# Closing a kernel's context behind its first three loads, and clearing its semaphores during the last store

## The chip, the cores and the metric

The kernel runs on one core of a Trainium2 chip. The metric is the device time of one execution, in microseconds. The core has five engines with a queue of instructions each: TensorE (PE in the profile; its weight loads are PEld), VectorE (DVE), ScalarE (ACT), GpSimd (POOL) and SyncE (SP). They run independently and wait for each other by semaphores, which are counters that one instruction raises and another waits for. SP and ACT issue transfers between the chip's memory and the on-chip buffers; 16 DMA engines carry them out, and each finished transfer raises a semaphore by 16.

## The reference: one decoding step of gated attention beside a gated feed-forward layer

One token with 512 features goes through an attention block that reads a cache of 32768 positions, and through a feed-forward block; a scalar gate mixes the two. All numbers are float32.

```
g   = sigmoid(sum(x * gate_w))                        # x: 1 x 1 x 512
q   = (x @ wq) as 32 heads of 128                     # wq: 512 x 4096
a   = softmax(q . k_cache * 128**-0.5) . v_cache      # 8 cached heads x 32768 x 128, four query heads share one
a   = a as 1 x 4096 @ wo                              # wo: 4096 x 512
b   = (silu(x @ w1) * (x @ w3)) @ w2                  # w1, w3: 512 x 1792, w2: 1792 x 512
out = g * a + (1 - g) * b                             # 1 x 1 x 512
```

The two caches are 134 MB each, the five weight matrices together 28 MB. Each is read once.

## The kernel before, in words

**Buffers.** Three large on-chip buffers, `ra`, `rb` and `rc`, hold 128 x 16384 numbers each (8.39 MB). They are reused in turn: first `rc` takes `wq`, `rb` takes `w1` and `w3`, and `ra` takes the first half of the first head's keys. Then `ra` and `rb` take the key halves of the eight heads and `rc` the value halves. At the end `ra` and `rb` take the last head's values, `rc` takes `wo`, and `ra` takes `w2` in four pieces.

**Loads.** All large loads are issued by SP, in the order in which they stand (lines 118 to 152). The first five (118 to 122) wait for nothing; line 124 waits until the feed-forward rows have read `rb` (the counter `c_e`), line 128 until the scores of the first key half are done (`c_k`), and so on. ACT issues the two small loads of `x` and `gate_w` (155, 156), a store of zeros to the output (162), and at the very end the store of the result (460). Both stores raise `l_out`.

**Work.** PE turns `x` into columns (187), computes the gate's sum (196), the queries (202) and the rows of the feed-forward layer (229). A loop over eight heads follows on PE and on DVE: DVE transposes keys (342), PE multiplies them with the queries (271), ACT takes the exponentials (386), PE multiplies with the values (285). The helper `take` (112) waits for a semaphore and lowers it again. Behind the loop come the products with `wo` (421) and `w2` (428, 438), the copies of the result (456), and the store.

**The frame.** The launch (lines 468 to 489) opens a context (485) and calls the kernel inside it. The kernel puts the whole program into one critical section of that context (line 27), inside which it sets all semaphores itself. The context and the section put instructions of their own around the program. In the profile they carry the line numbers 476 (the start of the program: every engine reports and is let go by POOL), 27 (the entry and the exit of the section) and 485 (a branch at the entry, and the end of the context: drains, semaphore instructions by which all engines report and are let go, and one instruction that clears a range of semaphores). A drain waits until an engine's earlier instructions are through. The last instruction of the program itself is line 461: POOL waits until both stores have landed.

Of the kernel before, what the change touches and what calls it, by code (L numbers as in the profile page):

```python
# [3 lines left out]
F32 = mybir.dt.float32  # L4
# [5 lines left out]
P = 128  # L10
# [13 lines left out]

@with_exitstack
def kernel(ctx, tc, x, k_cache, v_cache, wq, wo, w1, w3, w2, gate_w, out):
    with tc.tile_critical(sync_engine=mybir.EngineType.Activation, no_gpsimd_drain=True):
        _program(tc.nc, x, k_cache, v_cache, wq, wo, w1, w3, w2, gate_w, out)


def _program(nc, x, k_cache, v_cache, wq, wo, w1, w3, w2, gate_w, out):
    pe, dve, act, pool, sp = nc.tensor, nc.vector, nc.scalar, nc.gpsimd, nc.sync
    _, HKV, S, DH = k_cache.shape
    D = x.shape[-1]
    F = w1.shape[1]
    HQ = wq.shape[1] // DH
    REP = HQ // HKV
    NC = D // P
# [4 lines left out]
    W = NK * DH  # L43
    assert DH == P and D == 4 * P and REP == 4 and HKV == 8 and NK == 128 and F == FR * P

    def sb(name, *shape):
        return nc.alloc_sbuf_tensor(name, [P, *shape], F32).ap()

    def token(name):
        return nc.alloc_semaphore(name)  # L50

    def count(name):
        return Count(nc, name)


    ra, rb, rc = sb("ra", W), sb("rb", W), sb("rc", W)

    ident, ones, fold, dmask = sb("ident", P), sb("ones", P), sb("fold", 32), sb("dmask", 4)
    xp = sb("xp", NC, 32)
# [25 lines left out]
    def bank(n, w=1):  # L85
# [4 lines left out]
    pq = [bank(3), bank(4)]  # L90


    l_x, l_q = token("l_x"), token("l_q")
    l_a, l_a2, l_b, l_c = token("l_a"), token("l_a2"), token("l_b"), token("l_c")
    l_w1, l_w3 = token("l_w1"), token("l_w3")
    l_v = [token(f"l_v{i}") for i in range(2)]
    l_wo = [token(f"l_wo{i}") for i in range(2)]
    l_w2 = [token(f"l_w2{i}") for i in range(4)]
    l_out = token("l_out")

    c_q, c_k, c_v, c_e = (count(n) for n in ("c_q", "c_k", "c_v", "c_e"))
    c_nm, c_act, c_pool, done = token("c_nm"), count("c_act"), count("c_pool"), count("done")

    t_f, t_m, t_n, t_h, t_r, t_l = (token(n) for n in ("t_f", "t_m", "t_n", "t_h", "t_r", "t_l"))
    d_s = token("d_s")

    t_x, t_tr, t_win, t_ev, t_ob, t_mx, t_md, t_p, t_e = (
        token(n) for n in ("t_x", "t_tr", "t_win", "t_ev", "t_ob", "t_mx", "t_md", "t_p", "t_e")
    )

    def take(sem, n=1, engine=pe):
        engine.wait_ge(sem, n).then_inc(sem, -n)  # L112
# [2 lines left out]
    kd = k_cache.rearrange("a h (p m n) d -> (a h) m p (n d)", p=P, m=2, n=NK)  # L115
    vd = v_cache.rearrange("a h (r p n) d -> (a h) r p (n d)", r=2, p=P, n=NK)
    half = W // 2
    sp.dma_start(rc, wq.rearrange("(p c) n -> p (c n)", c=NC)).then_inc(l_q, 16)
    sp.dma_start(rb[:, 0:NC * F], w1.rearrange("(p c) f -> p (c f)", c=NC)).then_inc(l_w1, 16)
    sp.dma_start(rb[:, NC * F:2 * NC * F], w3.rearrange("(p c) f -> p (c f)", c=NC)).then_inc(l_w3, 16)  # L120
    sp.dma_start(ra[:, 0:half], kd[0, 0][:, 0:half]).then_inc(l_a, 16)
    sp.dma_start(ra[:, half:W], kd[0, 0][:, half:W]).then_inc(l_a2, 16)
    sp.wait_ge(c_e.sem, 2)
# [27 lines left out]
    for i in range(4):  # L151
# [17 lines left out]
        out=ident, in_=ident, compare_op=ALU.not_equal, fill=1.0, base=0, pattern=[[-1, P]], channel_multiplier=1,  # L169
# [256 lines left out]
    for k in range(W2[1]):  # L426
        t = k % 4
        i = pe.matmul(  # L428
            acc[32 * t:32 * t + 32, :], htp[:, k, :], w2t[:, k, :], start=False, stop=(k >= W2[1] - 4),
            skip_group_check=True,  # L430
        )
# [22 lines left out]
    for j in range(4):  # L454
        copy = act.copy if j % 2 else dve.tensor_copy
        i = copy(row[:, j * P:(j + 1) * P], pb[32 * j:32 * j + 1, 0:P])  # L456
# [1 line left out]
            done.by(i)  # L458
    act.wait_ge(done.sem, done.n)
    act.dma_start(od, row).then_inc(l_out, 16)  # L460
    c_pool.by(pool.wait_ge(l_out, 32))


# [26 lines left out]
```

## Time and profile before

| What | Value |
|---|---|
| median of 3 runs | 694.0 us (693.97 to 694.11) |
| the profiled execution | 694.02 us |
| its span, from the first to the last instruction of the program | 691.9 us |
| DMA queue of SP (q1) | 296.23 MB, 99.2% of 16 engines' span |
| mean rate over the span | 428 GB/s |
| busy: PE, DVE, ACT, POOL | 53%, 44%, 6%, 1% of the span |
| granted TensorE clock, mean | 0.785 |

In the rows shown below, times are microseconds from the span's start unless marked ns. A row of the timeline has the start, the duration, the engine, the line, the operation, what is written from what, the count, and in brackets the idle time before it with what ended it. A row of a line has the engine, the operation and the count, then the shortest, middle and longest duration in ns, and the starts of the first and the last. A small q behind an engine's name means its queue: drains, branches, semaphore instructions and the issue of a transfer, none of which counts as busy time. A row of stretches has start and end, the length, the busy time of each engine with its number of instructions, the granted TensorE clock, the mean busy share of the DMA engines and the rate.

### The profile page before, as it was taken

The numbers are of one execution on the slowest core, as the hardware profiler recorded it, in microseconds if no ns is written. First come the engines' busy times: TensorE is split into PE (matmuls) and PEld (weight loads), VectorE is DVE, ScalarE is ACT, GpSimd is POOL, SyncE is SP. The second block draws the span as 40 slices with busy tenths as digits, with TensorE's granted clock in tenths as the row PEclk, the third lists the DMA queues.
The fourth block names the chain that finished last, engine by engine and source line by source line (L and its number), as shares of the span: only waits on it lengthen the run. The fifth ranks groups of instructions, "written<-read, shape, count | busy, mean of one in ns | idle before, by whom it ended". The sixth has DMA issues, their size and how long they took to land. (4 is left out here: it accounts for less than half of the span.)

```text
span 691.9 us, 6738 instructions
## 1 busy us (share of the span) xinstructions
PE 368.2 (53%) x2952; PEld 107.5 (16%) x2952; DVE 307.0 (44%) x194; ACT 41.6 (6%) x111; POOL 7.0 (1%) x41
## 2 busy tenths in 40 slices
PE   1636255467463734466573735466463734466567
PEld 1100011103010121103010211103010211103122
DVE  1019378291725447091825446191816356181000
ACT  0020011002000010002000010001000010001000
POOL 0000000000000000000000000000000000000000
PEclk9975598868686977779577967888786966798678
DMA  9999999999999999999999999999999999999996
GB/s 383 421 439 454 424 429 425 447 447 424 425 432 432 436 447 436 424 424 432 432 440 451 428 424 428 436 428 443 447 424 424 432 432 436 447 436 424 424 423 291
DMA packets 6078, 296.35 MB, mean 428 GB/s; under 512 B 691, under 2 KB 691, under 8 KB 950
## 3 DMA queue, kind: packets, MB, share of 16 engines
q1 hardware_dynamic: 6048, 296.23, 99.2%
q8 instruction: 6, 0.10, 0.1%
q14 instruction: 2, 0.02, 0.0%
q10 hardware_dynamic: 22, 0.01, 0.0%
HBM read 296.23 MB, written 0.00 MB: 428 GB/s over the span
## 5 line engine op out<-in xcount | busy, mean ns | idle before, releaser
L342 DVE STREAM_TRANSPOSE rb<-rb 128x2048 f32<-128x2048 f32 x64 | 141.8, 2275 | 150.3 <-DVEq L112 150.3
L342 DVE STREAM_TRANSPOSE ra<-ra 128x2048 f32<-128x2048 f32 x64 | 141.4, 2275 | 43.6 <-DVEq L112 43.6
L271 PE MATMUL psum<-rb,winbuf 128*32 128x512 f32 x512 | 88.2, 766 | 130.2 <-PEq L112 130.2
L285 PE MATMUL psum<-rc,prob 128*32 128x512 f32 x896 | 111.2, 653 | 42.5 <-PEq L112 42.5
L271 PE MATMUL psum<-ra,winbuf 128*32 128x512 f32 x512 | 85.2, 764 | 86.7 <-PEq L112 86.7
L285 PEld LDWEIGHTS psum<-rc,prob 128*32 128x32 f32 x896 | 33.5, 120 | 115.5 <-issue 115.3
L366 DVE TENSOR_REDUCE mx<-psum 128x4 f32<-128x1024 f32 x8 | 9.8, 1224 | 81.6 <-DVEq L112 81.6
L271 PEld LDWEIGHTS psum<-rb,winbuf 128*32 128x32 f32 x512 | 13.1, 120 | 203.7 <-issue 203.7
L380 ACT COPY sbuf<-psum 128x512 f32<-128x512 f32 x16 | 9.8, 616 | 477.0 <-PE psum L271 477.0
L271 PEld LDWEIGHTS psum<-ra,winbuf 128*32 128x32 f32 x512 | 14.7, 121 | 150.1 <-issue 150.1
L386 ACT ACTIVATE prob<-psum,nm 128x256 f32<-128x256 f32 x32 | 18.8, 694 | 39.6 <-DVE nm L374 39.6
L295 PE MATMUL psum<-ident,sbuf 128*64 128x64 f32 x512 | 16.7, 223 | 0.8 <-PEq L112 0.8
L295 PEld LDWEIGHTS psum<-ident,sbuf 128*64 128x64 f32 x512 | 15.6, 138 | 7.6 <-issue 7.6
L347 DVE SCALAR_TENSOR_TENSOR otall<-psum,gate,recip 128x4 f32 (+1 forms) x8 | 1.7, 213 | 33.1 <-DVEq L112 33.1
L202 PE MATMUL psum<-rc,xp 128*32 128x512 f32 x64 | 9.8, 783 | 9.2 <-DMA rc<-in_A_wq_dram 9.2
L285 PE MATMUL psum<-rb,prob 128*32 128x512 f32 x64 | 8.4, 684 | 9.8 <-DMA rb<-in_A_v_cache_dram 9.8
L421 PE MATMUL psum<-rc,oq 128*32 128x512 f32 x64 | 10.7, 829 | 2.5 <-DMA rc<-in_A_wo_dram 2.1
L258 POOL COPY winbuf<-winraw 32x16 f32<-32x16 f32 x32 | 6.1, 189 | 537.2 <-PE psum L271 499.6
L285 PE MATMUL psum<-ra,prob 128*32 128x512 f32 x64 | 9.5, 761 | 3.7 <-DMA ra<-in_A_v_cache_dram 3.7
L229 PE MATMUL psum<-rb,xp 128*32 128x448 f32 x64 | 8.4, 683 | 5.6 <-DMA rb<-in_B_w_dram 5.6
L214 DVE STREAM_TRANSPOSE rc<-psum 128x512 f32<-128x512 f32 x2 | 1.3, 696 | 18.7 <-PE psum L202 18.7
L305 PE MATMUL psum<-fold,ob 128*128 128x4 f32 x64 | 8.4, 255 | 0.8 <-PEq L112 0.8
(62 smaller groups left out, 80.6 us busy)
## 6 DMA issues: line engine op xcount, KB each, us to landing
ra<-in_A_k_cache_dram SPq DMA_DIRECT2D x2, 4096.0 KB, 53.3
rc<-in_A_wo_dram SPq DMA_DIRECT2D x2, 4096.0 KB, 45.9
rb<-in_B_w_dram SPq DMA_DIRECT2D x2, 3584.0 KB, 34.7
ra<-in_B_w_dram SPq DMA_DIRECT2D x1, 1536.0 KB, 32.8
ra<-in_B_w_dram SPq DMA_DIRECT2D x1, 1024.0 KB, 35.0
ra<-in_B_w_dram SPq DMA_DIRECT2D x1, 768.0 KB, 36.3
ra<-in_B_w_dram SPq DMA_DIRECT2D x1, 256.0 KB, 36.5
rc<-in_A_v_cache_dram SPq DMA_DIRECT2D x14, 30.6
```

The lines of the kernel that those rows point to most:

```text
L202: m = pe.matmul(pq[b][32 * j:32 * j + 32, :], xp[:, c, :], rc[:, o:o + REP * DH], start=(c == 0), stop=(c == NC - 1),)
L229: i = pe.matmul(ps[32 * j:32 * j + 32, 0:FJ], xp[:, c, :], rb[:, o:o + FJ], start=(c == 0), stop=(c == NC - 1))
L258: pool.tensor_copy(winbuf[32 * r:32 * r + 32, 16:144].rearrange("p (c k) -> p c k", k=32)[:, :, 4 * r:4 * r + REP], winraw[32 * r:32 * r + ...
L271: i = pe.matmul(s_ps[m][32 * g:32 * g + 32, :], winbuf[:, w:w + 32], region.rearrange("p (n c i) -> p c n i", c=4, i=32)[:, c, n:n + 16], ...
L285: i = pe.matmul(o_ps[32 * t:32 * t + 32, :], prob[:, w:w + 32], region[:, n * DH:(n + 4) * DH], start=(r == 0 and g == 0 and f == 0), stop ...
L295: i = pe.matmul(pf[64 * s:64 * s + 64, 64 * a:64 * a + 64], sbuf[:, a].rearrange("p i m -> p (i m)"), ident.rearrange("p (gf r s q) -> p s ...
L305: i = pe.matmul(mb[:, 0:REP], ob[:, b * P:(b + 1) * P], fold[:, 4 * b:4 * b + 4], start=(b == 0), stop=(b == 3))
L342: dve.transpose(part[:, c], part[:, c]).then_inc(t_tr, 1)
L366: dve.tensor_reduce(mx, pf.rearrange("p (a q) -> p q a", q=REP), axis=AX.X, op=ALU.max).then_inc(t_mx, 1)
L380: act.copy(sbuf[:, :, :, m], s_ps[m].rearrange("p (n i) -> p n i", i=32)).then_inc(t_ev, 1)
L386: act.activation(prob[:, 0:1024].rearrange("p (a n q) -> p n a q", a=16, q=REP)[:, :, :, q], pf.rearrange("p (n a q) -> p n a q", n=16, q= ...
L421: pe.matmul(acc[32 * t:32 * t + 32, :], oq[:, k:k + 32], rc[:, k * D:(k + 1) * D], start=(k < 4), stop=False, skip_group_check=True,)
```

## The change

The context no longer encloses the program. The kernel allocates `rb` and `rc` and three semaphores, issues the loads of `wq`, `w1` and `w3` on SP, and closes and compiles the context at that point; these loads are marked as carrying no semaphore of the context itself. The program follows outside the context, with no critical section. It begins with the load of the first keys. At the end ACT signals `t_end` once it has issued the store; POOL waits for that, clears and frees all semaphores but `l_out`, and then waits for `l_out` and lowers it by 32.

```diff
 @with_exitstack
 def tile_gated_mix_decode_kernel(ctx, tc, x, k_cache, v_cache, wq, wo, w1, w3, w2, gate_w, out):
-    with tc.tile_critical(sync_engine=mybir.EngineType.Activation, no_gpsimd_drain=True):
-        _program(tc.nc, x, k_cache, v_cache, wq, wo, w1, w3, w2, gate_w, out)
-
-
-def _program(nc, x, k_cache, v_cache, wq, wo, w1, w3, w2, gate_w, out):
+    nc = tc.nc
+    rb, rc = (nc.alloc_sbuf_tensor(n, [P, 16384], F32).ap() for n in ("rb", "rc"))
+    l_q, l_w1, l_w3 = (nc.alloc_semaphore(n) for n in ("l_q", "l_w1", "l_w3"))
+    loads = [(rc, wq, l_q)]
+    n = w1.shape[0] * w1.shape[1] // P
+    loads += [(rb[:, i * n:(i + 1) * n], w, sem) for i, (w, sem) in enumerate(((w1, l_w1), (w3, l_w3)))]
+    for to, w, sem in loads:
+        i = nc.sync.dma_start(to, w.rearrange("(p c) n -> p (c n)", p=P)).then_inc(sem, 16)
+
+        tc.no_tile_sem_insts.add(i.ins.name)
+    tc.close()
+    tc.compile()
+    _program(nc, rb, rc, l_q, l_w1, l_w3, x, k_cache, v_cache, wq, wo, w1, w3, w2, gate_w, out)
+
+
+def _program(nc, rb, rc, l_q, l_w1, l_w3, x, k_cache, v_cache, wq, wo, w1, w3, w2, gate_w, out):
...
+    before = nc.snapshot_sems()
+
+
+    ra = sb("ra", W)
...
-    l_x, l_q = token("l_x"), token("l_q")
+    l_x = token("l_x")
     l_a, l_a2, l_b, l_c = token("l_a"), token("l_a2"), token("l_b"), token("l_c")
-    l_w1, l_w3 = token("l_w1"), token("l_w3")
...
-    l_out = token("l_out")
...
-    d_s = token("d_s")
+    d_s, t_end = token("d_s"), token("t_end")
...
+    owned = nc.allocated_since(before)
+    l_out = token("l_out")
...
-    sp.dma_start(rc, wq.rearrange("(p c) n -> p (c n)", c=NC)).then_inc(l_q, 16)
-    sp.dma_start(rb[:, 0:NC * F], w1.rearrange("(p c) f -> p (c f)", c=NC)).then_inc(l_w1, 16)
-    sp.dma_start(rb[:, NC * F:2 * NC * F], w3.rearrange("(p c) f -> p (c f)", c=NC)).then_inc(l_w3, 16)
     sp.dma_start(ra[:, 0:half], kd[0, 0][:, 0:half]).then_inc(l_a, 16)
...
     act.wait_ge(done.sem, done.n)
     act.dma_start(od, row).then_inc(l_out, 16)
-    c_pool.by(pool.wait_ge(l_out, 32))
+
+
+    act.wait_ge(done.sem, done.n).then_inc(t_end, 1)
+    pool.wait_ge(t_end, 1)
+    nc.clear_and_free_semaphores([l_q, l_w1, l_w3, *owned])
+    take(l_out, 32, pool)
```

More of the change, by code (lines that the diff above doesn't have):

```diff
@@ L53, in count @@
         return Count(nc, name)
-    ra, rb, rc = sb("ra", W), sb("rb", W), sb("rc", W)
+    before = nc.snapshot_sems()
+    ra = sb("ra", W)
     ident, ones, fold, dmask = sb("ident", P), sb("ones", P), sb("fold", 32), sb("dmask", 4)
```

## The prediction

> **What bounds the kernel now.** I read the page first: span, busy shares, the slices, the queues.
>
> ```profile
> span 691.9 us, 6738 instructions
> PE 368.2 (53%) x2952; PEld 107.5 (16%) x2952; DVE 307.0 (44%) x194; ACT 41.6 (6%) x111; POOL 7.0 (1%) x41
> DMA  9999999999999999999999999999999999999996
> q1 hardware_dynamic: 6048, 296.23, 99.2%
> q8 instruction: 6, 0.10, 0.1%
> ```
>
> No engine is busy for much over half of the span, while SP's queue (q1) fills 99.2% of the time of all 16 DMA engines: 296.23 MB of weights and cache are read once. So the kernel is a stream. Its time is the time before the first packet, then the stream, then what follows the last packet. The second view, busy time by stage, says where the stream is whole:
>
> ```profile
> core 0: us, PE busy (x) PEld busy (x) DVE busy (x) ACT busy (x) POOL busy (x), PEclk, DMA share, GB/s
> 0.00:4.00 4.00, 0.00 (x0) 0.00 (x0) 1.14 (x5) 1.23 (x1) 0.99 (x9) 1.00 0.81 263
> 4.00:42.00 38.00, 16.12 (x110) 5.94 (x114) 3.61 (x7) 4.64 (x19) 0.76 (x4) 0.96 0.99 427
> 42.00:62.00 20.00, 11.14 (x64) 1.98 (x56) 11.69 (x7) 0.00 (x0) 0.00 (x0) 0.66 1.03 444
> 62.00:120.00 58.00, 28.75 (x209) 6.38 (x213) 40.24 (x22) 4.88 (x11) 0.76 (x4) 0.74 1.00 431
> 120.00:660.00 540.00, 287.94 (x2355) 84.53 (x2347) 249.03 (x150) 29.21 (x77) 4.55 (x24) 0.78 1.00 433
> 660.00:689.20 29.20, 24.24 (x222) 8.71 (x222) 0.70 (x3) 1.17 (x2) 0.00 (x0) 0.83 0.91 386
> 689.20:691.90 2.70, 0.00 (x0) 0.00 (x0) 0.56 (x2) 0.52 (x2) 0.00 (x0) 1.00 0.00 1
> ```
>
> The DMA share is 0.99 to 1.03 from 4 us to 660 us: there is no hole that the change could fill, so what happens between the first loads and the last ones is worth nothing unless it opens a hole. The first 4 us and the last 2.7 us are what the change can touch; in the last 2.7 us the DMA engines do nothing (share 0.00) and the other engines work for half a microsecond. I read the end from the chain of waits, the timeline, the lines of the closing instructions, and the waits of the queue engines, one view after the other:
>
> ```profile
> 687.09 2.12 PE psum L438 x68
> ```
> ```profile
> 689.85 0.21 ACTq L460 DMA_DIRECT2D out_dram<-prob  x1
> ```
> ```profile
> L461 POOLq EVENT_SEMAPHORE  x1: 17/17/17, 691.0 to 691.0; - x1
> ```
> ```profile
> L27 ACTq EVENT_SEMAPHORE  x3: 17/38/38, 690.1 to 690.5; - x3
> L27 ACTq DRAIN  x1: 158/158/158, 690.2 to 690.2; - x1
> ```
> ```profile
> L485 SPq EVENT_SEMAPHORE  x4: 17/22/73, 690.2 to 691.8; - x4
> L485 POOLq EVENT_SEMAPHORE  x4: 17/17/17, 691.2 to 691.7; - x4
> L485 POOLq DRAIN  x3: 34/41/64, 691.1 to 691.6; - x3
> L485 PEldq EVENT_SEMAPHORE  x2: 51/51/51, 691.4 to 691.8; - x2
> L485 POOLq EVENT_SEMAPHORE_RANGE_CLEAR  x1: 71/71/71, 691.5 to 691.5; - x1
> ```
> ```profile
> SPq L485 <- POOLq L27: 0.7, 1, 0.7
> ```
>
> The last matrix products end at 689.2, the store is issued at 689.85, and POOL sees it landed at 691.0 (L461): the store covers about 1.1 us. Only then comes what line 485, the end of the context, has: three drains on POOL, two rounds in which every engine reports and is let go, and between them one clear of the semaphores (71 ns). SP stands 0.7 us for POOL in the meantime. From 691.0 to the span's end at 691.9 nothing of the program's work is done.
>
> **The change part by part.** The sum is made against the profiled execution, 694.02 us, of which 691.9 is span and 2.1 lies outside; the median of the three runs is 694.0, so nothing need be converted.
>
> *The end.* The closing goes from behind the store. What follows the store's landing is one POOL instruction, the wait that also takes the 32 back (17 ns, as L461 has it now, in the same place). Saved: 691.9 - 691.0 = 0.9 us. The rows round to a tenth, so 0.8 to 1.0.
>
> *The clear under the store.* ACT signals t_end behind the issue of the store, in the place where it has a semaphore instruction at 690.1 now; nothing is queued behind that wait on ACT. POOL waits for it, and behind POOL's wait stand the clear and the last wait. By the rows above a drain on each side of the clear costs at most 64 ns and the clear 71: about 0.2 us, twice that if the numbers fall into two ranges. POOL is through by 690.3 to 690.6, and the store lands at 691.0. I cost it at nothing; the cover is the store, and without it the price is 0.2 to 0.4 us.
>
> *The start of the stream.* The lines of the first microsecond, and behind them the timeline:
>
> ```profile
> L476 SPq EVENT_SEMAPHORE  x1: 17/17/17, 0.7 to 0.7; - x1
> ```
> ```profile
> L27 ACTq NOP  x1: 18/18/18, 0.7 to 0.7; - x1
> ```
> ```profile
> L485 SPq COMPARE_BRANCH  x1: 33/33/33, 0.8 to 0.8; - x1
> ```
> ```profile
> 0.92 0.37 SPq L118 DMA_DIRECT2D rc<-in_A_wq_dram  x1
> 0.97 0.53 ACTq L155 DMA_DIRECT2D ob<-in_A_x_dram  x1
> 1.54 0.73 ACTq L156 DMA_DIRECT2D prob<-in_gate_w_dram  x1
> 1.82 0.42 SPq L120 DMA_DIRECT2D rb<-in_B_w_dram  x1
> 2.29 0.53 SPq L121 DMA_DIRECT2D ra<-in_A_k_cache_dram  x1
> 10.74 2.02 PE L187 MATMUL psum<-ones,ob 1*128 1x1 f32 x8 [10.74 <-DMA prob<-in_gate_w_dram]
> 13.11 0.55 PE L196 MATMUL psum<-gsm,ones 1*128 1x1 f32 x2 [0.35 <-PEq L112]
> 22.82 7.69 PE L202 MATMUL psum<-rc,xp 128*32 128x512 f32 x44 [9.15 <-DMA rc<-in_A_wq_dram]
> 41.30 5.27 PE L229 MATMUL psum<-rb,xp 128*32 128x448 f32 x32 [5.64 <-DMA rb<-in_B_w_dram]
> ```
>
> SP is let go by the launch's own barrier at 0.7 (L476), takes a branch at 0.8 that ACT's NOP of line 27, the entry of the section, releases, and issues the first load at 0.92. Outside the section that release is gone; the branch may stay. The load can come between 0.72, right behind the barrier, and 0.92 as now: a gain of 0 to 0.2, and a loss of 0.1 if the context's own entry puts one more branch there. I take 0.1, the middle of the gain, since either end needs one of the two instructions wholly gone or wholly kept. As the stream has no hole up to 660, an earlier first packet is an earlier last one.
>
> *The closing at the front.* It is now paid behind the third load. SP ends that issue at 1.82 + 0.42 = 2.24, less 0.1; the two rounds with the clear cost 0.9 as at the end; so every engine starts on the rest at about 3.0. SP's fourth load goes from 2.29 to about 3.1. Cover: the three loads hold 8.39 + 3.67 + 3.67 = 15.7 MB, 37 us at 427 GB/s; 0.8 us costs nothing. The drains do not wait for the loads: at the end ACT's drain took 158 ns at 690.2 with its store in flight until 691.0. ACT's two small loads go from 0.97 and 1.54 to about 3.0 and 3.6, DVE's and POOL's constants with them. PE then has x at 12.8 instead of 10.74 and is done with the gate at 15.7 instead of 13.66, against the landing of wq at 22.82: of 9.15 us of idle time 2.1 go. Should the small loads take twice their 9.2 us (1.54 to 10.74) because the stream is now ahead of them, PE starts on wq about 2 us late. What is late next is SP's queue:
>
> ```profile
> 46.64 0.33 SPq L124 DMA_DIRECT2D rb<-in_A_k_cache_dram  x1
> 71.06 0.33 SPq L128 DMA_DIRECT2D ra<-in_A_k_cache_dram  x1
> ```
>
> The first five loads are 24.1 MB, 56.5 us, so they last until about 58, and L124 is issued at 46.64, 12 us ahead; its 8.39 MB last until about 78, and L128 is issued at 71.06, 7 us ahead. Two microseconds fit into both. Price: nothing; ends 0 and 2.
>
> *The rest.* Fewer entries of the section, other semaphore numbers, rb and rc allocated ahead of ra: no row shows a price of an address or a number, and I take none.
>
> Sum: 694.02 - 0.9 - 0.1 = 693.0 us, 0.14% less.
>
> **The rivals.**
>
> *The time outside the span shrinks too.* All five engines now leave together at 691.8, the last semaphore rows of line 485. After the change PE is done at 689.2, ACT and POOL at 690.9 at the latest. 2.1 us lie outside the span; if part of it is work that each engine does by itself after its last instruction, and the slow one is PE (51 ns for a semaphore instruction against 17 on POOL), the end moves by more than POOL's: by up to the 1.6 us that PE is now ahead of POOL, half of the 2.1 at most if half lies behind the span. I price it at 0.4 to 1.1: 691.9 to 692.6, middle 692.3. For it speaks that nothing holds the four engines any longer; against it, that no row shows what the 2.1 us are. The Trainium skill, "Runtime: NRT & Kernel Launch", section "The ~15µs preamble/postamble breakdown", has a barrier behind the kernel in which all engines are waited for, about 1.5 us, ahead of the reset of the semaphores: by that rule the early engines would wait for POOL, nothing more is gained, and the time stays 693.0. The profile shows no instruction of it.
>
> *The closing waits for the loads.* This is the way to a slower kernel. If the context's end holds the engines until the three loads have landed, the barrier opens at 42 us: the second half of L229, the third load's reader, starts at 41.30, and the closing takes 0.9. SP issues its fourth load then, 2 us behind the end of the three (about 2 + 37), and refilling the queue takes about 1 (the first load is issued at 0.92, and by the share of 0.81 0.8 of the first 4 us is empty): 3 us lost. x is asked for at 42, and from x to the issue of L124 lie 36 us now (10.74 to 46.64), of which the waits for the first and the third load (9.15 and 5.64) would be gone: about 21. So L124 would come at 42 + 21 and 2 to 9 for x, 65 to 72, where the fourth and fifth load are through at 43 + 20 = 63: another 3 to 10. Together 6 to 13 lost, 1 gained: 699 to 706, middle 702. It decides from the point where the barrier opens more than about 9 us late, past PE's idle time before wq, and more than 7 past that. For it speaks that a context's end is a place of waits; against it, that the loads are marked as carrying none of the context's own semaphores, and the ACT drain above.
>
> *A code fetch falls on the last load.* Six packets of q8 bring instructions: 0.1% of 16 x 691.9 us is 11 us, 1.8 each (0.9 to 2.8 with the rounding), on one DMA engine that then delivers its share of the stream late. The closing's instructions now stand ahead of PE's work, so each fetch comes a few instructions earlier. If one moves onto the engine that brings the last part of w2, the end is 1.8 later: 694.8. The Trainium skill's "Runtime: NRT & Kernel Launch", section "Instruction fetch mechanics", gives blocks of 16 KiB, 256 instructions; q8's six packets with 0.10 MB agree, and a shift of a few in 256 then leaves nearly every fetch at the same work.
>
> *It doesn't do what it says*: leaving the launch's block still runs a closing. Then the end stays and 694.0 remains.
>
> **How the numbers follow.** About 0.2% (1.4 us) is what a measurement of this kernel can tell from no change. Forecast as summed: 46%, at 693.0, own range 692.7 to 693.4, which is within 0.2%. More gained outside the span: 33%, 691.9 to 692.6, faster by over 0.2%. Closing waits for the loads: 10%, slower. Code fetch: 7%, of which 5 within 0.2% and 2 slower. Nothing done: 4%, within. So faster 0.33, within 0.55, slower 0.12. The range from 691.9 to 694.1 holds the forecast, the first rival and the last, 83%.
>
> **What would show it.** Right: the span ends with POOL's wait at about 690.9, no row of line 485 or of the clear behind the store's landing, span 690.9; the first load at 0.8; the barrier rows at 2.2 to 3.0; PE at x near 13 and still idle before wq; the DMA share 0.99 or more from 4 to 660. The first rival: the run's time minus its span clearly under 2.1. The second: barrier rows at 40, a hole in the DMA shares there. The third: the stage behind 660 longer with L438 later against the stream. What would make me wrong most likely is the time outside the span, of which the trace of before shows nothing.

## The result, and the profile after

The changed kernel takes 692.67 us (median of 18 runs, 692.47 to 692.90) against 694.01 for the kernel before, a ratio of 0.9981 with a 95% interval of 0.9974 to 0.9987: 1.34 us less. The forecast was 693.0. The profiled execution took 692.64 us.

The page, and the stages where the stream must show a hole if there is one (columns as in the prediction):

```profile
span 690.7 us, 6722 instructions
q1 hardware_dynamic: 6048, 296.23, 99.3%
q8 instruction: 6, 0.10, 0.1%
```
```profile
4.00:42.00 38.00, 16.00 (x114) 6.07 (x118) 3.85 (x9) 5.87 (x19) 0.76 (x4) 0.94 0.99 427
42.00:62.00 20.00, 11.46 (x60) 1.75 (x52) 12.14 (x7) 0.00 (x0) 0.00 (x0) 0.69 1.03 444
62.00:120.00 58.00, 29.13 (x217) 6.60 (x221) 40.39 (x23) 4.89 (x11) 0.76 (x4) 0.76 1.00 431
120.00:660.00 540.00, 294.60 (x2350) 84.70 (x2339) 248.42 (x149) 29.27 (x77) 4.55 (x24) 0.76 1.00 433
```

The DMA shares and rates are those of before to the last digit: nothing changed in the middle. The start, first the lines of the closing (line 38 now), then the timeline:

```profile
L38 POOLq EVENT_SEMAPHORE  x4: 17/17/17, 2.3 to 2.7; - x4
L38 SPq DRAIN  x3: 7/7/122, 2.1 to 2.5; - x3
```
```profile
0.73 0.37 SPq L34 DMA_DIRECT2D rc<-in_A_wq_dram  x1
1.16 0.90 SPq L34 DMA_DIRECT2D rb<-in_B_w_dram  x2
2.84 0.33 SPq L131 DMA_DIRECT2D ra<-in_A_k_cache_dram  x1
2.86 0.52 ACTq L165 DMA_DIRECT2D ob<-in_A_x_dram  x1
3.42 0.73 ACTq L166 DMA_DIRECT2D prob<-in_gate_w_dram  x1
```
```profile
15.33 2.02 PE L197 MATMUL psum<-ones,ob 1*128 1x1 f32 x8 [15.33 <-DMA prob<-in_gate_w_dram]
17.71 0.55 PE L206 MATMUL psum<-gsm,ones 1*128 1x1 f32 x2 [0.35 <-PEq L125]
22.81 9.26 PE L212 MATMUL psum<-rc,xp 128*32 128x512 f32 x64 [4.55 <-DMA rc<-in_A_wq_dram]
```

The first load is issued at 0.73 instead of 0.92. Behind the third load come the two rounds of the closing, done at 2.8, with no clear between them; then everything else starts. x is there at 15.33 instead of 10.74, and PE still stands 4.55 us for wq and begins on it at 22.81, as before. The end, from the timeline and the lines:

```profile
689.51 0.21 ACTq L470 DMA_DIRECT2D out_dram<-prob  x1
```
```profile
L475 POOLq DRAIN  x1: 110/110/110, 689.8 to 689.8; - x1
L475 POOLq EVENT_SEMAPHORE_RANGE_CLEAR  x1: 265/265/265, 690.0 to 690.0; - x1
```
```profile
L125 POOLq EVENT_SEMAPHORE  x1: 17/17/17, 690.6 to 690.6; - x1
```

The store is issued at 689.51, POOL drains and clears at 689.8 to 690.3, and the wait for the store passes at 690.6, 1.1 us behind its issue as before. It is the last instruction: the closing that filled 691.0 to 691.9 is gone. In these two executions the store is issued 0.34 us earlier (689.51 against 689.85), more than the first load's 0.19; the rest is the size of what single executions differ by, whose spans lie between 690.6 and 691.0 in the changed kernel.

Each run lists its time and its span, so the difference can be taken over all runs. This table has the mean span and the mean of time minus span for every kernel (the spans are given to 0.1 us, the means over 8 to 32 runs are good to a few hundredths; the last kernel has 4 runs). Two executions that took far longer, one of before (1092.24 us) and one of e3 (718.35 us), are left out of the means. The kernel before ran again beside every later set of experiments and took 694.02 to 694.07 us there, with 2.17 to 2.20 us outside the span, so the rows can be compared across the sets to within some 0.06 us.

| Kernel | time, median us | ratio, 95% interval | span | outside the span |
|---|---|---|---|---|
| before (beside the first four experiments) | 694.01 | | 691.83 | 2.19 |
| changed | 692.67 | 0.9981 (0.9974 to 0.9987) | 690.76 | 1.92 |
| e1, closing put back at the end | 693.87 | 0.9997 (0.9988 to 1.0007) | 691.79 | 2.07 |
| e2, closed ahead of the loads | 693.36 | 0.9992 (0.9983 to 1.0001) | 691.47 | 1.93 |
| e3, cleared behind the store | 693.21 | 0.9988 (0.9979 to 0.9998) | 691.33 | 1.90 |
| e4, all five engines end together | 692.99 | 0.9985 (0.9976 to 0.9994) | 690.86 | 2.16 |
| e5, PE has the last wait | 692.46 | 0.9978 (0.9969 to 0.9987) | 690.82 | 1.67 |
| e6, SP has the last wait | 692.16 | 0.9973 (0.9963 to 0.9984) | 690.76 | 1.43 |
| e7, ACT has the last wait | 692.33 | 0.9976 (0.9967 to 0.9986) | 690.81 | 1.54 |
| e8, DVE has the last wait | 692.21 | 0.9975 (0.9965 to 0.9985) | 690.79 | 1.47 |
| e11, SP waits, cleared early | 692.30 | 0.9975 (0.9966 to 0.9984) | 690.95 | 1.38 |
| e10, x late | 692.70 | 0.9980 (0.9971 to 0.9989) | 690.76 | 1.91 |
| e12, PE's code shifted | 692.73 | 0.9980 (0.9971 to 0.9989) | 690.81 | 1.88 |
| e9, front waits for its loads | 703.31 | 1.0138 (1.0123 to 1.0154) | 701.50 | 1.92 |

So the 1.34 us are 1.07 in the span (0.9 at the end and 0.19 at the start, by the rows above) and 0.27 outside it.

### The profile page after: what moved, and what is told of

Its sections match the earlier page's. It is cut to its first block, busy times and chain, and to the rows that moved or that the text cites. A ratio compares the mean times of both kernels' runs of the same rounds, so it can differ in the third digit from the quotient of the medians.

```text
span 690.7 us, 6722 instructions
## 1 busy us (share of the span) xinstructions
PE 376.6 (55%) x2952; PEld 107.8 (16%) x2952; DVE 307.0 (44%) x194; ACT 41.7 (6%) x111; POOL 7.1 (1%) x41
## 5 line engine op out<-in xcount | busy, mean ns | idle before, releaser
L281 PE MATMUL psum<-rb,winbuf 128*32 128x512 f32 x512 | 96.3, 833 | 123.6 <-PEq L125 123.6
L295 PE MATMUL psum<-rc,prob 128*32 128x512 f32 x896 | 113.0, 661 | 41.3 <-PEq L125 41.3
L197 PE MATMUL psum<-ones,ob 1*128 1x1 f32 x8 | 2.0, 370 | 15.3 <-DMA prob<-in_gate_w_dram 15.3
```

The costliest lines, as they stand in the source:

```text
L281: i = pe.matmul(s_ps[m][32 * g:32 * g + 32, :], winbuf[:, w:w + 32], region.rearrange("p (n c i) -> p c n i", c=4, i=32)[:, c, n:n + 16], ...
L295: i = pe.matmul(o_ps[32 * t:32 * t + 32, :], prob[:, w:w + 32], region[:, n * DH:(n + 4) * DH], start=(r == 0 and g == 0 and f == 0), stop ...
```

## The experiments

All are edits of the changed kernel, whose closing lines are these:

```
act.wait_ge(done.sem, done.n).then_inc(t_end, 1)
pool.wait_ge(t_end, 1)
nc.clear_and_free_semaphores([l_q, l_w1, l_w3, *owned])
take(l_out, 32, pool)
```

### e1: the closing back at the end

```diff
-    nc.clear_and_free_semaphores([l_q, l_w1, l_w3, *owned])
     take(l_out, 32, pool)
+    nc.all_engine_barrier()
+    nc.clear_and_free_semaphores([l_q, l_w1, l_w3, *owned])
+    nc.all_engine_barrier()
```

> The changed kernel with a closing put back behind the store's landing: two rounds in which all engines report, the clear between them. Theory (the end gives 0.86 us, the start 0.19, the time outside the span the rest, because four engines leave early): the span grows by 0.7 to 0.9 us, the time outside it goes back from 1.9 to about 2.15, so 693.5 to 693.8 us. Rival (most of the gain comes from the front, by the earlier loads and the other addresses of the buffers): 692.7 to 693.2 us.

693.87 us. The lines at the end, where 477 is the clear and 478 the second round:

```profile
L125 POOLq EVENT_SEMAPHORE  x1: 42/42/42, 690.8 to 690.8; - x1
```
```profile
L477 POOLq EVENT_SEMAPHORE_RANGE_CLEAR  x1: 265/265/265, 691.3 to 691.3; - x1
L478 SPq EVENT_SEMAPHORE  x1: 17/17/17, 691.8 to 691.8; - x1
```

From the store's landing at 690.8 to the last round at 691.8 lies 1.0 us, and the time outside the span grows by 0.15. With its closing at the end the kernel is only 0.14 us faster than before, and the interval holds 1: the end, not the front, carries most of the gain. The time is 0.07 above the upper end of what was expected. This closing is longer than that of before (1.0 us against 0.9), and its clear takes 265 ns where that of before took 71.

### e2: closed ahead of the loads

```diff
-    for to, w, sem in loads:
-        i = nc.sync.dma_start(to, w.rearrange("(p c) n -> p (c n)", p=P)).then_inc(sem, 16)
-        tc.no_tile_sem_insts.add(i.ins.name)
     tc.close()
     tc.compile()
+    for to, w, sem in loads:
+        nc.sync.dma_start(to, w.rearrange("(p c) n -> p (c n)", p=P)).then_inc(sem, 16)
```

> The changed kernel with the context closed first and the three loads issued behind it. Theory (the stream has no hole, so its end moves with its first packet): the first load goes from 0.73 to about 1.4 us, everything up to the store moves by 0.7, so 693.3 to 693.4 us. Rival (the start of the stream doesn't count, the last microseconds are set by PE): 692.7 us, no change.

693.36 us. The timeline's first load:

```profile
1.39 0.37 SPq L36 DMA_DIRECT2D rc<-in_A_wq_dram  x1
```

The first load is 0.66 us later (1.39 against 0.73) and the kernel 0.69 slower. The start of the stream is paid in full at its end. The rival, that PE sets the end, falls. The page of the kernel before seems to speak for it, since the last chain there, from 672.6 to 689.2, is PE's. But the records of landings show that the last piece of w2 lands at 688.67 there, at 688.35 in the changed kernel and at 689.13 in e2, and the store of the result is issued 1.17 to 1.18 us behind it each time: the end follows the stream.

### e3: cleared behind the store

```diff
-    nc.clear_and_free_semaphores([l_q, l_w1, l_w3, *owned])
     take(l_out, 32, pool)
+    nc.clear_and_free_semaphores([l_q, l_w1, l_w3, *owned])
```

> The changed kernel with the clear behind POOL's wait for the store instead of ahead of it. Theory (the store's flight hides the clear): the drain and the clear now lie open, with the durations that they have in the changed kernel (110 and 265 ns, 0.4 us with the gaps): 693.0 to 693.1 us. Rival (they took that long only because the store was under way; alone they cost 41 and 71 ns as in the kernel before): 692.8 to 692.9 us.

693.21 us, 0.54 more than the changed kernel and 0.11 above the upper end of what was expected. The lines:

```profile
L125 POOLq EVENT_SEMAPHORE  x1: 43/43/43, 690.7 to 690.7; - x1
```
```profile
L476 POOLq DRAIN  x1: 110/110/110, 690.8 to 690.8; - x1
L476 POOLq EVENT_SEMAPHORE_RANGE_CLEAR  x1: 265/265/265, 690.9 to 690.9; - x1
```

Drain and clear take 110 and 265 ns with no store in flight, just as with one, so the store does not slow them; they are longer than the 34 to 64 and 71 ns of before for another reason, which was not tried (in e11 the list holds three semaphores fewer and the clear takes 244 ns). Hiding them under the store is worth half a microsecond here.

### e4: all five engines end together

```diff
     nc.clear_and_free_semaphores([l_q, l_w1, l_w3, *owned])
+    pool.wait_ge(l_out, 32).then_inc(leave, 4)
     take(l_out, 32, pool)
+    for engine in (pe, dve, act, sp):
+        take(leave, 1, engine)
```

> The changed kernel with one more wait at the end of PE, DVE, ACT and SP, for a semaphore that POOL raises once the store has landed, so that all five engines end together again. Theory (the time outside the span shrank because four engines now end earlier): span longer by 0.1 us, time outside the span back from 1.9 to about 2.15, so 692.95 to 693.1 us. Rival (what lies outside the span has another reason and stays at 1.9): 692.75 to 692.8 us.

692.99 us: 0.1 in the span (690.86 against 690.76) and 0.24 outside it (2.16 against 1.92). PE's last instruction, one wait, is the only thing it does behind its last product:

```profile
L126 PEldq EVENT_SEMAPHORE  x1: 51/51/51, 690.9 to 690.9; - x1
```

The time outside the span comes back when the five engines end together: 0.24 of the 0.27 us. So the gain outside the span comes from four engines ending earlier than the last one.

### e5 to e8: another engine has the last wait

```diff
-    take(l_out, 32, pool)
+    take(l_out, 32, pe)      # e5; sp in e6, act in e7, dve in e8
```

> The changed kernel with the last wait, for the store, on PE instead of POOL; POOL ends with the clear. The four kernels of this set differ in nothing but the engine that ends last. Theory (what lies outside the span holds work that each engine does by itself behind its last instruction, and PE's is the longest, since its semaphore instructions take 51 ns against 17 to 21): the time outside the span is 2.15 to 2.2 as before, 692.9 to 693.0 us. Rival (another engine, or the meeting of several, sets it): 1.9, 692.7 us.

> The changed kernel with the last wait on SP. Theory (PE's share outside the span is the longest and POOL's no shorter than SP's): the time outside the span is 1.9 or less, 692.4 to 692.7 us. Rival (SP's share is the long one): 2.15, 692.95 us.

> The changed kernel with the last wait on ACT, which also issues the store. Theory: the time outside the span is 1.9 or less, 692.4 to 692.7 us. Rival (ACT's share is the long one): 2.15, 692.95 us.

> The changed kernel with the last wait on DVE. Theory: the time outside the span is 1.9 or less, 692.4 to 692.7 us. Rival (DVE's share is the long one): 2.15, 692.95 us.

The spans are equal within 0.06 us (690.76 to 690.82), and the times differ: PE 692.46, ACT 692.33, DVE 692.21, SP 692.16, against 692.67 with POOL. All four lie below what was expected, PE by 0.44 us and the others by 0.07 to 0.24. SP's row in e6 stands where POOL's stood:

```profile
L125 SPq EVENT_SEMAPHORE  x1: 17/17/17, 690.7 to 690.7; - x1
```

My theory that PE's share outside the span is the longest is wrong: with PE last 1.67 us lie outside, with POOL last 1.92. Whichever single engine ends last, less is paid than when all do (1.43 to 1.92 against 2.16), so the share of the slowest engine alone doesn't explain the time outside either. e6 beats both kernels: 1.85 us less than before, 0.51 less than the changed kernel.

### e11: SP waits, and POOL clears before the store

```diff
...
-    act.wait_ge(done.sem, done.n)
+    take(done.sem, done.n, act)
     act.dma_start(od, row).then_inc(l_out, 16)
-    act.wait_ge(done.sem, done.n).then_inc(t_end, 1)
-    pool.wait_ge(t_end, 1)
+    pool.wait_ge(c_e.sem, n_ff + 3).then_inc(t_end, 1)
     nc.clear_and_free_semaphores([l_q, l_w1, l_w3, *owned])   # owned without c_e, done, t_end
-    take(l_out, 32, pool)
+    take(t_end, 1, sp)
+    take(l_out, 32, sp)
+    take(c_e.sem, n_ff + 3, sp)
```

> The changed kernel with the last wait on SP, as in the run where SP waits, and with POOL's clear moved ahead of the store, to the end of PE's work; the counters still in use then (c_e, done, t_end) are left out of the clear and lowered by their last reader. Theory (behind its last instruction each engine has work of its own, POOL's 1.9 us and the longest; with SP waiting, POOL, done at 690.3, still sets the end at 692.2): POOL is done at 689.3, and the time falls below 692.1, to 691.3 at the lowest. Rival (SP's own work is 1.4 us and sets the end there): 692.2 us, no gain over the run where SP waits.

692.30 us. The lines of POOL's clear and of SP's waits:

```profile
L473 POOLq EVENT_SEMAPHORE_RANGE_CLEAR  x1: 244/244/244, 689.1 to 689.1; - x1
```
```profile
L126 SPq EVENT_SEMAPHORE  x3: 17/17/17, 689.0 to 690.8; - x3
```

POOL is done at 689.4, 0.9 us sooner than in e6, and the time did not fall. The rival's mechanism held, at 0.1 us above its figure: in e6 the end is not POOL's any more, and 1.4 us outside the span is what remains with SP last. It is 0.14 slower than e6, no more than its longer span accounts for (690.95 against 690.76). SP has one more wait behind the store here, ACT lowers `done` ahead of the store (issued 1.26 us behind the last landing, against 1.18 in e6), and the kernel before also took 0.06 us longer beside e11 than beside e6.

### e10 and e9: how much the front can bear

```diff
+    act.wait_ge(l_q, 16)                       # e10, ahead of ACT's loads of x and gate_w
```
```diff
+    for engine in (sp, act, dve, pool, pe):    # e9, ahead of SP's fourth load
+        engine.wait_ge(l_w3, 16)
```

> The changed kernel with ACT's two small loads held until wq has landed, at 22.8 instead of 2.9 us. x comes at about 35 and PE starts on wq some 15 us late. Theory (PE's idle time before wq and SP's lead over the stream together hold about 16 us): the stream has no hole or a very short one, 692.7 to 693.7 us. Rival (a late x is paid in full or in half): 699 to 708 us.

> The changed kernel in which all five engines stand behind the closing until the third load has landed, at 41 us: what the context's end would cost if it waited for its loads. By the prediction's working 6 to 13 us are lost against the changed kernel: the fourth load comes into an empty queue (3), and line 134's load is issued behind the end of the fifth (3 to 10): 699 to 706 us. Rival (only the empty queue at 41 costs): 695 to 696 us.

e10 took 692.70 us, no more than the changed kernel. Its timeline, ACT's load of x, PE's x, PE's start on wq and SP's sixth load:

```profile
22.70 0.52 ACTq L166 DMA_DIRECT2D ob<-in_A_x_dram  x1
```
```profile
30.98 2.02 PE L198 MATMUL psum<-ones,ob 1*128 1x1 f32 x8 [30.98 <-DMA prob<-in_gate_w_dram]
33.83 8.44 PE L213 MATMUL psum<-rc,xp 128*32 128x512 f32 x64
```
```profile
48.35 0.33 SPq L134 DMA_DIRECT2D rb<-in_A_k_cache_dram  x1
```

x is asked for 20 us later, PE starts on wq 11 us later (33.83 against 22.81), and the load of the next keys goes out at 48.35 instead of 45.83, only 2.5 us later: PE no longer stands for the third load. The stream has data until about 58, so there is no hole.

e9 took 703.31 us, 10.6 more than the changed kernel. Its stages and SP's sixth load:

```profile
38.00:41.00 3.00, 0.00 (x0) 0.00 (x0) 1.15 (x5) 0.00 (x0) 0.79 (x5) 1.00 0.66 195
41.00:60.00 19.00, 12.13 (x90) 5.15 (x94) 2.84 (x6) 1.45 (x2) 0.00 (x0) 1.00 0.96 414
60.00:66.00 6.00, 4.77 (x52) 1.32 (x44) 1.18 (x3) 4.45 (x17) 0.76 (x4) 1.00 0.47 156
```
```profile
64.84 0.33 SPq L136 DMA_DIRECT2D rb<-in_A_k_cache_dram  x1
```

Here the stream runs dry twice: the rate is 195 GB/s between 38 and 41 us, where the engines are let go at 39.6, and 156 between 60 and 66, where the next load comes at 64.84. This is what a closing that waits for its loads would have cost, and it lies within the 699 to 706 us that the prediction worked out for that rival.

### e12: PE's instruction blocks shifted

```diff
+    for _ in range(100):
+        pe.drain()                             # ahead of PE's wait for x
```

> The changed kernel with 100 drains more at the head of PE's instructions, ahead of its wait for x, where PE is idle until 15 us. Every later fetch of PE's instructions (the packets of q8, one at 687.4 us in the changed kernel) comes 100 instructions earlier, among the last pieces of w2 instead of at their end. Theory (where PE's instruction blocks end doesn't matter beyond some tenths): 692.5 to 692.9 us. Rival (the code fetch on the engine that brings the last piece, priced at 1.8 us in the prediction): 693.5 to 694.5 us.

692.73 us, no change. The page's queue row and the line of the drains:

```profile
q8 instruction: 6, 0.10, 0.1%
```
```profile
L195 PEldq DRAIN  x100: 7/8/8, 2.9 to 9.9; - x100
```

There are still six fetches, each of them 100 instructions earlier in PE's work; the last starts at 683.3 instead of 687.4 by the trace's packet records. The last piece of w2 lands at 688.3 in both kernels. In the changed kernel the last fetch (687.4 to 688.5) was still under way when that piece landed, and in e12 (683.3 to 684.4) it was long done. Neither place shows in the time. The records used here don't say on which of the 16 DMA engines the fetch ran.

## Why the prediction was right or wrong

The time lies in the range, the change is below 0.2% as the likeliest case had it, and the sum was 0.3 us short. The range is wide because it takes in the first rival: 692.67 is just under the sum's own range (692.7 to 693.4) and just above that rival's (691.9 to 692.6), and the runs show some of both. The forecast took 0.2% as the least that a measurement could tell; 0.19% was told, since the interval stays below 1. By its steps:

- *The end*, 0.9 forecast: right. 691.0 to 691.9 before, 690.6 to 690.7 after; e1 puts 1.0 back.
- *The clear under the store*, costed at nothing: right, and its price without cover was 0.2 to 0.4 by the forecast and 0.54 by e3. The rows of before gave too short a drain and clear (64 and 71 ns against 110 and 265).
- *The start of the stream*, 0.1 forecast out of 0 to 0.2: mis-sized. The load comes at 0.73 right behind the barrier: the branch went altogether, and 0.19 us are gained. e2 shows that such a shift is paid one for one.
- *The closing at the front*, costed at nothing: right. It ended at 2.8 where 3.0 was expected. x came at 15.3 where 12.8 was expected: the second small load takes 11.9 us (3.42 to 15.33), against 9.2 before. Why stays open; in e10, with the stream in full run, it takes 7.7 (23.27 to 30.98). 4.6 us of PE's idle time still covered the delay. e10 shows that much more would have fitted.
- *The rest*, taken as nothing: nothing is left over for it. The rows of the end and the start make 0.9 + 0.19 = 1.09 us, and the span fell by 1.07.
- *The time outside the span*, taken as fixed at 2.1: this is the step that failed. It fell by 0.27 us. The first rival had the mechanism, and e4 confirms it, but it was priced too high (0.4 to 1.1), and its reason was wrong: it made PE the slow engine because a semaphore instruction takes 51 ns there, and e5 shows that with PE last less is paid than with POOL last. The rule drawn from the Trainium skill's "Runtime: NRT & Kernel Launch", section "The ~15µs preamble/postamble breakdown" (a barrier for all engines, so early engines gain nothing) doesn't hold for this time: it depends on how many engines end last and on which.
- *Closing that waits for its loads*: didn't happen; its price was right (e9).
- *The code fetch*: no sign of it (e12). By the packet records of the changed kernel a fetch takes 0.9 to 1.1 us, the low end of the forecast's working (1.8, 0.9 to 2.8 with the rounding).

What the 1.4 to 2.2 us outside the span consist of stays open: the trace shows no instruction there.

## What to carry to other kernels

Where one transfer queue is full from the first load to the last, look at the few microseconds in front of the first packet and behind the last one: barriers there are paid in full, and in front of work that the stream already covers they cost nothing. Behind the last transfer let one engine wait and the others end, and choose that engine by trial: on this kernel it was worth another 0.5 us to let SP wait instead of POOL. Before putting a barrier in front, work out how long the loads ahead of it last and how late the first reader may be.

## What the runs showed of the hardware

Time that no instruction in the trace accounts for depends on which engine ends last: 1.92 us with POOL, 1.67 with PE, 1.54 with ACT, 1.47 with DVE, 1.43 with SP, 2.16 with all five. The second of ACT's two loads of 2 KB, issued while SP's loads were under way, let PE start 7.7 to 11.9 us later (1.54 to 10.74 before, 3.42 to 15.33 in the changed kernel, 23.27 to 30.98 in e10). SP's drain behind its three loads took 122 ns with all of them in flight.
